# A gated long convolution and a SwiGLU layer on one core: the block convolution rewritten with four tokens per partition, the FFN weights kept in SBUF

## The chip, the cores and the metric

The kernel runs on one core of one Trainium2 chip. A core has several engines that run beside each other, each with its own queue of instructions in a fixed order, and they wait for one another through semaphores: TensorE (PE in the profile; its weight loads are listed as PEld), VectorE (DVE), ScalarE (ACT), GpSimd (POOL) and SyncE (SP). In this kernel SP and POOL only start transfers, apart from a few small memory fills on POOL. Matrix products land in PSUM, a small memory divided into banks, from which DVE or ACT carry the result to SBUF, the core's working memory; the inputs, the output and some intermediate arrays lie in DRAM.

The metric is the device time of one execution, in microseconds. Before the change the median of three runs is 397.13 us (397.08 to 398.56).

## The reference: what is computed

There are 2048 tokens of width D = 640 and an FFN of width F = 1728, all in bf16. With `x = A_q`:

```
k_shift[t] = sum over j in 0..3 of k[t-j] * shift_k[:, j]
kv   = k_shift * v
y    = causal convolution of kv along the tokens with ssm_k (2048 taps per channel)
y    = y + kv * ssm_D
h    = x + layernorm(x) * y
out  = h + (silu(n @ w_gate) * (n @ w_up)) @ w_down      with n = layernorm(h)
```

The reference writes the convolution with FFTs of length 4096. Both kernels cut the tokens into four blocks of 512 and the filter into four pieces of 512, transform each by a matrix product with a fixed table of cosines and sines, multiply the spectra of block j and filter piece p elementwise, add the products for output block i = j + p, and transform back by another matrix product. Ten (j, p) pairs are needed.

## The kernel before, in words

The program is written with a tile library: the text gives the operations in order and names buffers from pools; when the program is built, a scheduler puts the instructions of each engine into one fixed order. Where an operation's buffer is free and its operands are ready in the scheduler's own time, an operation that stands later in the text can go ahead of an earlier one. A buffer is free again when every reader of what it held is done.

*Filter pieces* (`g_piece`, L189). A piece is loaded, transposed on PE in sixteen rounds of five (L196), copied by ACT (L197) and transformed by `fwd_transform` (L147): eight groups of 4x2 matmuls of 320 columns (L153), each evacuated by ACT (L155). Pieces 1 to 3 are combined with the piece before by `hbuild` (L178, two DVE operations of 2560 elements a partition) and written to DRAM.

*Block front* (`conv_front_tiles`, L234). A block of 512 tokens is four tiles of 128 tokens, one token per partition. For each tile SP loads x, four copies of k shifted by 0 to 3 tokens (L250, L252; for the very first tile the shifted copies begin at partition 1, 2 or 3) and v. ACT takes the sums for the layer norm (L124, L125), DVE forms kv in eight operations of 640 elements (L257 to L262). `conv_front_finish` normalises x on ACT (L139) and transforms kv (L153).

*Products* (`cmac`, L157). A spectrum is 1024 coefficients by 640 channels, 8x640 elements per partition, and a pair is six or eight DVE operations of 2560 elements. The products go forward: as soon as the spectrum of block j exists, `pair(j, pp)` adds it to the accumulator of each later block; all accumulators stay in SBUF, and the filter spectra 1 to 3 are read back from DRAM (L226).

*Block back* (`conv_back`, L287). The inverse transform (L303) takes 16 matmuls of 320 columns per tile; DVE multiplies the PSUM result by the normalised x (L306) and adds x, loaded a second time (L313). h goes to DRAM (L314). ACT takes the sums of h, a square root (L134) and the normalisation (L139); PE transposes (L335) and ACT copies the result to hlnT (L336).

*FFN* (`ffn_quarter`, L338). POOL loads the gate and up weights again for each of the four blocks, in seven groups. For each of 14 chunks of up to 128 hidden units PE does five gate and five up matmuls of 512 columns (L356, L358) into one PSUM bank each; ACT makes the sigmoid, a copy of gate and a copy of up (L360 to L364), DVE two products (L366, L367). The down projection is 28 matmuls of 320 columns per tile (L376); DVE adds h, which POOL has loaded back from DRAM (L379, L381), and POOL stores the result (L382).

*Order in the text* (L384 to L405): front and back of block 0 with filter piece 0, pieces 1 to 3, then for k = 1, 2, 3: front of block k, back of block k, FFN of block k-1, the remaining forward products of block k-1; at last FFN 3. SP issues nearly all loads and the stores of spectra and h, in that order; POOL issues the FFN weights, h and the output.

Of the kernel before, what the change touches and what calls it, by code (L numbers as in the profile page):

```python
# [10 lines left out]
DEBUG_OUT = "out"  # L11

FP32 = mybir.dt.float32
BF16 = mybir.dt.bfloat16
ACT = mybir.ActivationFunctionType
# [3 lines left out]
D = 640  # L19
FF = 1728  # L20
P = 128
NT = S_TOT // P
MBLK = 512
NB = S_TOT // MBLK
TT_PER_BLK = MBLK // P
L = 2 * MBLK
NCOEF = 1024
NCT = NCOEF // P
EPS = 1e-5
NFCH = 14  # L30
GRP = 2
NGRP = NFCH // GRP
NH = 320


def make_basis():
    k = np.arange(MBLK)
    n = np.arange(MBLK)
    theta = 2 * np.pi * np.outer(k + 0.5, n) / L
    WF = np.concatenate([np.cos(theta), np.sin(theta)], axis=0).T.copy()  # L40
    WI = (2.0 / L) * np.concatenate([np.cos(theta), np.sin(theta)], axis=0)
    return WF.astype(np.float32), WI.astype(np.float32)
# [3 lines left out]
def kernel(  # L46
# [20 lines left out]
    cpool = ctx.enter_context(tc.tile_pool(name="cpool", bufs=1))  # L67
    ident_h = nc.inline_tensor(np.eye(P, dtype=np.float32).astype(ml_dtypes.bfloat16), name="const_ident")
    ident = cpool.tile([P, P], BF16, name="ident")
    nc.sync.dma_start(out=ident[:], in_=ident_h.ap())  # L70
    w4 = cpool.tile([P, 4, D], BF16, name="w4")
    with tc.tile_pool(name="tmpw", bufs=1) as tmpw:
        wbig = tmpw.tile([P, D, 4], BF16, name="wbig")
        nc.sync.dma_start(out=wbig[:], in_=A_shift_k.partition_broadcast(P))
        for j in range(4):
            nc.vector.tensor_copy(w4[:, j, :], wbig[:, :, j])
    wdp = ctx.enter_context(tc.tile_pool(name="wdp", bufs=1))
    freq = ctx.enter_context(tc.tile_pool(name="freq", bufs=1))
    blk = ctx.enter_context(tc.tile_pool(name="blk", bufs=1))
    iop = ctx.enter_context(tc.tile_pool(name="iop", bufs=2))  # L80
    ffq = ctx.enter_context(tc.tile_pool(name="ffq", bufs=1))
    wst = ctx.enter_context(tc.tile_pool(name="wst", bufs=2))
    ffio = ctx.enter_context(tc.tile_pool(name="ffio", bufs=2))
    small = ctx.enter_context(tc.tile_pool(name="small", bufs=2))
    dram = ctx.enter_context(tc.tile_pool(name="dram", bufs=1, space=bass.MemoryType.DRAM))
    psA = ctx.enter_context(tc.tile_pool(name="psA", bufs=2, space=bass.MemoryType.PSUM))
    psG = ctx.enter_context(tc.tile_pool(name="psG", bufs=1, space=bass.MemoryType.PSUM))
    psT = ctx.enter_context(tc.tile_pool(name="psT", bufs=2, space=bass.MemoryType.PSUM))
    gst0 = blk.tile([P, 5, MBLK], BF16, name="gst")
    nc.sync.dma_start(out=gst0[:], in_=A_ssm_k[0:D, 0:MBLK].rearrange("(dc p) t -> p dc t", p=P))  # L90

    WFnp, WInp = make_basis()
    WF_h = nc.inline_tensor(WFnp.astype(ml_dtypes.bfloat16), name="const_wf")
    WI_h = nc.inline_tensor(WInp.astype(ml_dtypes.bfloat16), name="const_wi")
    sgn_np = np.array([1.0 if (p % 2) == 0 else -1.0 for p in range(P)], dtype=np.float32).reshape(P, 1)
    sgn_h = nc.inline_tensor(sgn_np, name="const_sgn")
    nsgn_h = nc.inline_tensor((-sgn_np).astype(np.float32), name="const_nsgn")
    sgn_t = cpool.tile([P, 1], FP32, name="sgn_t")
    nc.sync.dma_start(out=sgn_t[:], in_=sgn_h.ap())
    nsgn_t = cpool.tile([P, 1], FP32, name="nsgn_t")  # L100
    nc.sync.dma_start(out=nsgn_t[:], in_=nsgn_h.ap())
    eps_t = cpool.tile([P, 1], FP32, name="eps_t")
    nc.vector.memset(eps_t[:], EPS)
    zero_t = cpool.tile([P, 1], FP32, name="zero_t")
    nc.vector.memset(zero_t[:], 0.0)
    Drow = cpool.tile([1, D], BF16, name="Drow")
    nc.sync.dma_start(out=Drow[:], in_=A_ssm_D.partition_broadcast(1))
    WF_t = cpool.tile([P, TT_PER_BLK, NCOEF], BF16, name="WF_t")
    WI_t = cpool.tile([P, NCT, MBLK], BF16, name="WI_t")

    wd_sb = wdp.tile([P, NFCH, D], BF16, name="wd_sb")

    h_dram = dram.tile([S_TOT, D], BF16, name="h_dram")
    hf_dram = dram.tile([NB, P, NCT, D], BF16, name="hf_dram")
    graw_dram = dram.tile([NB, P, NCT, D], BF16, name="graw_dram")

    Aacc = [freq.tile([P, NCT, D], BF16, name=f"Acc{i}") for i in range(NB)]
    Xcur = freq.tile([P, NCT, D], BF16, name="Xcur")
    Hld = [freq.tile([P, NCT, D], BF16, name=f"Hld{i}") for i in range(2)]
    Tprod = freq.tile([P, 4, D], BF16, name="Tprod")  # L120

    def ln_stats(x_tile: bass.AP, mv_out: bass.AP):
        junk = iop.tile([P, D], BF16, name="junk", bufs=1)
        nc.scalar.activation(junk[:], x_tile, ACT.Identity, bias=zero_t[:], scale=1.0, accum_out=mv_out[:, 0:1])  # L124
        nc.scalar.activation(junk[:], x_tile, ACT.Square, accum_out=mv_out[:, 1:2])  # L125

    def ln_finish_block(mvb: bass.AP, rb: bass.AP, nbb: bass.AP):
        T = mvb.shape[1]
        nc.vector.tensor_scalar(mvb[:, :, 0:1], mvb[:, :, 0:1], 1.0 / D, None, op0=ALU.mult)
        msq = small.tile([P, T, 1], FP32, name="ln_msq")  # L130
        nc.vector.tensor_mul(msq[:], mvb[:, :, 0:1], mvb[:, :, 0:1])
        nc.vector.scalar_tensor_tensor(mvb[:, :, 1:2], mvb[:, :, 1:2], 1.0 / D, msq[:], op0=ALU.mult, op1=ALU.subtract)
        sb = small.tile([P, T, 1], FP32, name="ln_sb")
        nc.scalar.activation(sb[:], mvb[:, :, 1:2], ACT.Sqrt, bias=eps_t[:], scale=1.0)  # L134
        nc.vector.reciprocal(rb, sb[:])
        nc.vector.scalar_tensor_tensor(nbb, mvb[:, :, 0:1], -1.0, rb, op0=ALU.mult, op1=ALU.mult)

    def ln_apply(x_tile: bass.AP, out_ap: bass.AP, rcol: bass.AP, nbcol: bass.AP):
        nc.scalar.activation(out_ap, x_tile, ACT.Identity, bias=nbcol, scale=rcol)  # L139

    def ps3(ps: bass.AP) -> bass.AP:
        return ps[:, :, 0:NH]

    def r3(ap2d: bass.AP) -> bass.AP:
        return ap2d.rearrange("p (a b) -> p a b", a=2)

    def fwd_transform(src4: bass.AP, dst8: bass.AP):  # L147
        for ct in range(NCT):
            ps = psA.tile([P, 2, 512], FP32, name="ps_mm")
            for kt in range(TT_PER_BLK):  # L150
                lhsT = WF_t[:, kt, ct * P:(ct + 1) * P]
                for h in range(2):
                    nc.tensor.matmul(ps[:, h, 0:NH], lhsT, src4[:, kt, h * NH:(h + 1) * NH],  # L153
# [35 lines left out]
    def g_piece(p: int, gst=None):  # L189
        if gst is None:  # L190
            gst = g_load(p)
# [244 lines left out]
```

## Time and profile before

| what | value |
|---|---|
| median of 3 runs | 397.13 us (397.08 to 398.56) |
| the profiled execution, first to last instruction | 397.7 us (no other time is listed for it) |
| mean granted TensorE clock | 0.955 |
| moved by DMA | 68.91 MB, mean 173 GB/s |
| first transform matmul / first FFN matmul / last matmul | 25.9 / 79.3 / 393.1 us |
| matmul records, weight loads | 1914, 1936 |

The profile page gives the busy time of each engine and the span in 40 slices of about 10 us, a digit being the busy share in tenths. A table by stages gives for each stretch of time the length, the busy time and number of instructions of PE, PEld, DVE, ACT and POOL, the mean granted clock, the DMA share and GB/s. In a timeline a line has the start, the length, the engine, the line of the program, the operation, output and inputs with their shape, and how many neighbours are merged. "128x640" is partitions by elements per partition; the engines' times follow the second number. "SPq" is SP's queue at work on issuing a transfer.

### The profile page before, as it was taken

How to read it: one execution, taken by the hardware profiler on the slowest of the kernel's cores; microseconds unless marked ns; L12 is line 12 of the kernel's file. 1: busy time of each engine (PE TensorE's matmuls, PEld its weight loads, DVE VectorE, ACT ScalarE, POOL GpSimd, SP SyncE). 2: the span in 40 equal slices, each digit the busy share in tenths (PEclk: the TensorE clock that was granted, in tenths of full speed). 3: DMA queues.
4: the chain of work that ended last, by engine and by line, in shares of the span. 5: the costliest groups of instructions: out<-in, count | busy, mean ns of one | idle time of the engine just before them, and what ended most of it. 6: DMA issues, size and time to landing. Idle time of an engine off the chain costs nothing.

```text
span 397.7 us, 5429 instructions
## 1 busy us (share of the span) xinstructions
PE 325.7 (82%) x1914; PEld 185.3 (47%) x1936; DVE 254.7 (64%) x413; ACT 253.8 (64%) x447; POOL 68.1 (17%) x95
## 2 busy tenths in 40 slices
PE   1038874497899779999779899897998999999995
PEld 1025542364567324565354355454534554544463
DVE  1185498500629989999949999983699723233321
ACT  1259607999786636479987539976664697166610
POOL 5000001000000303203102211131131111433121
PEclk9999969589999969999999999989999999999999
DMA  8589847513886996366863716351043332254111
GB/s 249 180 314 357 296 146 242 157 66 109 321 303 259 356 335 218 101 178 220 305 190 101 266 49 199 104 155 56 16 141 106 112 96 77 100 155 142 52 51 49
DMA packets 33610, 68.91 MB, mean 173 GB/s; under 512 B 4213, under 2 KB 25904, under 8 KB 31920
## 3 DMA queue, kind: packets, MB, share of 16 engines
q1 hardware_dynamic: 26800, 45.63, 33.7%
q0 software_dynamic: 6784, 22.94, 18.5%
q8 instruction: 15, 0.25, 0.2%
q14 instruction: 11, 0.09, 0.1%
HBM read 56.77 MB, written 11.80 MB: 172 GB/s over the span
## 4 chain that ended last, share of the span: by engine, by line
PE 33%; issue 25%; ACT 14%; DMA 13%; DVE 11%; SPq 2%; POOL 2%; POOLq 0%; DVEq 0%; ACTq 0%
PE ps_g L356 11%; PE ps_mm L376 7%; PE ps_mm L153 6%; PE ps_u L358 6%; PE ps_mm L303 4%; DMA wu_g<-in_B_w_up_dram 3%; ACT gc L362 3%; ACT xln_blk L139 3%; DMA k_148<-in_A_k_dram 2%; DMA wg_g<-in_B_w_gate_dram 2%; ACT junk L124 2%; SPq L250 2%; ACT sig L360 2%; DMA WF_t<-const_wf 1%; DMA wbig<-in_A_shift_k_dram 1%
## 5 line engine op out<-in xcount | busy, mean ns | idle before, releaser
L356 PE MATMUL ps_g<-hlnT,wg_g 128*128 128x512 bf16 (+1 forms) x268 | 70.9, 386 | 11.1 <-DMA wg_g<-in_B_w_gate_dram 6.1
L153 PEld LDWEIGHTS <-WF_t 128*128 128x128 bf16 x512 | 51.3, 101 | 48.7 <-DMA WF_t<-const_wf 13.8
L358 PE MATMUL ps_u<-hlnT,wu_g 128*128 128x512 bf16 (+1 forms) x270 | 70.3, 384 | 2.0 <-ACT uc L364 1.3
L376 PE MATMUL ps_mm<-wd_sb,tT 128*128 128x320 bf16 x448 | 69.6, 302 | 1.0 <-DVE tT L367 1.0
L360 ACT ACTIVATE sig<-ps_g 128x512 bf16<-128x512 f32 (+1 forms) x56 | 33.4, 597 | 50.0 <-PE ps_g L356 44.5
L376 PEld LDWEIGHTS <-tT 128*128 128x128 bf16 x448 | 41.9, 98 | 25.6 <-issue 7.1
L346 POOL DMA_DIRECT2D wg_g<-in_B_w_gate_dram x28 | 24.4, 873 | 168.9 <-PE ps_g L356 156.2
L153 PE MATMUL ps_mm<-gT,WF_t 128*128 128x320 bf16 x256 | 40.8, 313 | 15.1 <-DMA WF_t<-const_wf 13.5
L356 PEld LDWEIGHTS <-wg_g 128*128 128x128 bf16 (+1 forms) x280 | 27.3, 99 | 47.4 <-issue 14.7
L153 PE MATMUL ps_mm<-kv_blk,WF_t 128*128 128x320 bf16 x256 | 39.0, 307 | 6.9 <-ACT Xcur L155 3.9
L358 PEld LDWEIGHTS <-wu_g 128*128 128x128 bf16 (+1 forms) x280 | 27.5, 99 | 34.6 <-issue 3.7
L366 DVE TENSOR_TENSOR gs<-gc,sig 128x512 bf16<-128x512 bf16 (+1 forms) x56 | 23.2, 419 | 30.3 <-ACT gc L362 30.3
L364 ACT CAST uc<-ps_u 128x512 bf16<-128x512 f32 (+1 forms) x56 | 32.8, 586 | 10.8 <-DVE tT L367 3.3
L303 PEld LDWEIGHTS <-WI_t 128*128 128x128 bf16 x256 | 25.8, 102 | 17.5 <-issue 5.3
L362 ACT CAST gc<-ps_g 128x512 bf16<-128x512 f32 (+1 forms) x56 | 32.6, 582 | 0.0
L348 POOL DMA_DIRECT2D wu_g<-in_B_w_up_dram x28 | 24.4, 871 | 34.1 <-PE ps_u L358 21.5
L367 DVE TENSOR_TENSOR tT<-gs,uc 128x512 bf16<-128x512 bf16 (+1 forms) x56 | 23.2, 419 | 7.3 <-ACT uc L364 7.0
L155 ACT CAST Xcur<-ps_mm 128x640 bf16<-128x640 f32 x32 | 21.7, 693 | 9.0 <-PE ps_mm L153 9.0
L124 ACT ACTIVATE junk<-h_t,zero_t 128x640 bf16<-128x640 bf16 x16 | 13.2, 828 | 21.8 <-DVE h_t L313 21.5
L261 DVE TENSOR_TENSOR kv_blk<-kv_blk,ktmp 128x640 bf16<-128x640 bf16 x48 | 23.4, 487 | 0.8
L124 ACT ACTIVATE junk<-x_t,zero_t 128x640 bf16<-128x640 bf16 x16 | 13.3, 831 | 13.0 <-DMA x_t<-in_A_q_dram 12.7
L382 POOL DMA_DIRECT2D out_dram<-o_t x16 | 8.8, 553 | 65.4 <-DVE o_t L381 52.0
(256 smaller groups left out, 412.7 us busy)
## 6 DMA issues: line engine op xcount, KB each, us to landing
wg_g<-in_B_w_gate_dram POOLq DMA_DIRECT2D x24, 320.0 KB, 3.6
wu_g<-in_B_w_up_dram POOLq DMA_DIRECT2D x24, 320.0 KB, 4.2
Hld_129<-hf_dram SPq DMA_DIRECT2D x3, 1280.0 KB, 5.5
Hld_130<-hf_dram SPq DMA_DIRECT2D x3, 1280.0 KB, 9.9
gst<-in_A_ssm_k_dram SPq DMA_DIRECT2D x4, 640.0 KB, 7.7
x_t<-in_A_q_dram SPq DMA_DIRECT2D x16, 160.0 KB, 5.4
v_t<-in_A_v_dram SPq DMA_DIRECT2D x16, 160.0 KB, 3.9
h_dram<-h_t SPq DMA_DIRECT2D x16, 160.0 KB, 2.7
```

The source lines that it names most:

```text
L124: nc.scalar.activation(junk[:], x_tile, ACT.Identity, bias=zero_t[:], scale=1.0, accum_out=mv_out[:, 0:1])
L153: nc.tensor.matmul(ps[:, h, 0:NH], lhsT, src4[:, kt, h * NH:(h + 1) * NH], start=(kt == 0), stop=(kt == TT_PER_BLK - 1))
L261: nc.vector.tensor_add(ks, ks, tmp[:])
L303: nc.tensor.matmul(ps[:, h, 0:NH], lhsT, Acc[:, ct, h * NH:(h + 1) * NH], start=(ct == 0), stop=(ct == NCT - 1))
L346: nc.gpsimd.dma_start(out=wg_g[:, :, 0:ncols], in_=B_w_gate[:, f0:f0 + ncols].rearrange("(kt p) f -> p kt f", p=P))
L348: nc.gpsimd.dma_start(out=wu_g[:, :, 0:ncols], in_=B_w_up[:, f0:f0 + ncols].rearrange("(kt p) f -> p kt f", p=P))
L356: nc.tensor.matmul(ps_g[:csz, :], wg_g[:, kt, off:off + csz], hlnT[:, kt, :], start=(kt == 0), stop=(kt == 4))
L358: nc.tensor.matmul(ps_u[:csz, :], wu_g[:, kt, off:off + csz], hlnT[:, kt, :], start=(kt == 0), stop=(kt == 4))
L360: nc.scalar.activation(sig[:csz, :], ps_g[:csz, :], ACT.Sigmoid)
L362: nc.scalar.copy(gc[:csz, :], ps_g[:csz, :])
L364: nc.scalar.copy(uc[:csz, :], ps_u[:csz, :])
L376: nc.tensor.matmul(ps_o[:, h, 0:NH], lhsT, wd_sb[:csz, c, h * NH:(h + 1) * NH], start=(c == 0), stop=(c == NFCH - 1))
```

## The change

The computation is the same; nearly all of the code is new. Lines of the new kernel, cut to what the text speaks of:

```diff
+    spp = pool("spp", 6)
+    ldp = pool("ldp", 4)
+    hp = pool("hp", 2)
+    psg = pool("psg", 3, space=bass.MemoryType.PSUM)
+    psm = pool("psm", 2, space=bass.MemoryType.PSUM)
+    pst = pool("pst", 1, space=bass.MemoryType.PSUM)
...
+    def kv_loads(b, hf):
...
+        kt = kvp.tile([P, 7, NH], BF16, name="kt")
+        if b == 0:
+            nc.gpsimd.memset(kt[0:1, 0:3, :], 0.0)
+            nc.sync.dma_start(out=kt[:, 3:7, :], in_=kk[0:BLK, d0:d0 + NH].rearrange("(p j) d -> p j d", j=4))
+            nc.sync.dma_start(out=kt[1:P, 0:3, :], in_=kk[0:BLK - 4, d0:d0 + NH].rearrange("(p j) d -> p j d", j=4)[:, 1:4, :])
+        else:
+            src = bass.AP(tensor=kk.tensor, offset=kk.offset + (r0 - 3) * D + d0, ap=[[4 * D, P], [D, 7], [1, NH]])
+            nc.sync.dma_start(out=kt[:], in_=src)
...
+    def fwd_split(src, dst):
+        eo = spp.tile([P, 2, 4, NH], BF16, name="eo", tag="sp")
+        for par in range(2):
+            for c in range(2):
+                ps = psm.tile([P, 2, 512], FP32, name="ps_f", tag="mm")
+                for q in range(2):
+                    for j in (par, par + 2):
+                        nc.tensor.matmul(ps[:, q, 0:NH], fwd_w(j, 0, c * 2 + q), src[:, j, :],
+                                         start=(j == par), stop=(j == par + 2))
+                nc.scalar.copy(eo[:, par, c * 2:c * 2 + 2, :], ps[:, :, 0:NH])
+        nc.vector.tensor_add(dst[:, 0:4, :], eo[:, 0], eo[:, 1])
+        nc.vector.tensor_sub(dst[:, 4:8, :], eo[:, 0], eo[:, 1])
...
+        nc.vector.tensor_scalar(rb.bitcast(I32), var[:].bitcast(I32), -0.5, 1597463007.0, op0=ALU.mult, op1=ALU.add)
+        for _ in range(3):
+            nc.vector.tensor_mul(t[:], rb, rb)
...
+    def g_transform(p, gst, dst2):
+        gT = hp.tile([P, NJ, D], BF16, name="gT", tag="xln")
...
+    def conv_half(b, hf):
...
+        kv = kv_make(b, hf, kvt[b, hf])
+        xc = spp.tile([P, 8, NH], BF16, name="xc", tag="sp")
+        if b == 0:
+            fwd_dense(kv, xc)
+        else:
+            fwd_split(kv, xc)
+        if b < NB - 1:
+            nc.gpsimd.dma_start(out=x_dr[b][hf], in_=xc[:])
+        acc = spp.tile([P, 8, NH], BF16, name="acc", tag="sp")
+        for j in range(b):
+            xl = ldp.tile([P, 8, NH], BF16, name="xl", tag="ld")
+            nc.sync.dma_start(out=xl[:], in_=x_dr[j][hf])
+            hl = ldp.tile([P, 8, NH], BF16, name="hl", tag="ld")
+            nc.sync.dma_start(out=hl[:], in_=h_dr[b - j][hf])
+            pair(acc, xl, hl, first=(j == 0))
+        pair(acc, xc, h0[hf], first=(b == 0))
+        xln = xln_b[b]
+        if b > 0:
+            ee = t2p.tile([P, 4, NH], BF16, name="ee", tag="t2")
+            nc.vector.tensor_add(ee[:], acc[:, 0:4, :], acc[:, 4:8, :])
+            nc.vector.tensor_sub(acc[:, 4:8, :], acc[:, 0:4, :], acc[:, 4:8, :])
...
+            nc.vector.tensor_scalar(hln[:], h_t[:, j, :], rb[:, j, :], nbb[:, j, :], op0=ALU.mult, op1=ALU.add)
...
+    def ffn(b):
...
+        for c in range(NC_FULL):
...
+            ps_g = psg.tile([P, BLK], FP32, name="ps_g", tag="gu")
...
+            ps_u = psg.tile([P, BLK], FP32, name="ps_u", tag="gu")
...
+            with tc.high_priority():
+                nc.scalar.activation(sil[:], ps_g[:], ACT.Silu)
+                nc.scalar.copy(uc[:], ps_u[:])
+                nc.vector.tensor_mul(tT[:, c, :], uc[:], sil[:])
...
+            if not last:
+                for h in range(2):
+                    nc.tensor.matmul(ps_o[:, h, 0:NH], ident[:], h_t[:, m, h * NH:(h + 1) * NH], start=True, stop=False)
...
+    for p in range(1, NB):
+        cur = [spp.tile([P, 8, NH], BF16, name="gc", tag="sp") for hf in range(2)]
+        g_transform(p, gt, cur)
+        h_build(p, cur, prev)
+        prev = cur
+        if p < NB - 1:
+            gt = g_load(p + 1)
+        if p == 1:
+            x_load(1)
+            ln1(1)
+            for hf in range(2):
+                conv_half(1, hf)
+            ln2(1)
+            ffn(0)
+    for b in range(2, NB):
+        x_load(b)
+        ln1(b)
+        for hf in range(2):
+            conv_half(b, hf)
+        ln2(b)
+        ffn(b - 1)
+    ffn(NB - 1)
```

What it does, part by part (the number in a pool is how many buffers a tag of it has):

- The tag `sp` (six buffers) holds raw filter pieces, even and odd halves, spectra and accumulators; `ld` (four) the spectra read back; `xln` (two) the transposed filter pieces and the normalised x, which turns into h in place and stays until the block's FFN has used it. Gate and up share three PSUM banks, transposes have one.
- In `conv_half`, `kv_make` and each of its products are DVE operations of 1280 elements (`pair`: six for the first product of a block, else eight). The full forward or inverse transform of a half takes 32 matmuls, the split one 16.
- A block's token 4p + j lies on partition p, place j. One load brings the seven k rows that a partition needs, and the width is worked in two halves of 320 (`hf`), each with its own transforms, products and inverse.
- The frequencies are shifted by a quarter step instead of a half. The upper half of the 512 complex frequencies then has the table of the lower half, with the sign of odd places j turned. `fwd_split` transforms even and odd places separately with half the matmuls and forms their sum and difference on DVE; the inverse likewise (`ee`). Block 0 and all filter pieces use the full form.
- The products go backward: block b reads the spectra of earlier blocks and of the filter pieces from DRAM when it needs them. Only piece 0's spectrum stays in SBUF.
- The gate, up and down weights are loaded once, by SP; the left-over 64 gate and up columns share one group of five matmuls. Stores of spectra (`h_build` for the filter pieces) and of the output go through POOL. Silu replaces sigmoid, copy and one product. h stays in SBUF; for blocks 0 to 2 it is added by two matmuls with the identity.
- The normalisation's inverse root is made by 15 small DVE operations (three Newton steps), h is normalised on DVE, and the four shift weights are copied apart by ACT.
- In the text, FFN 0 now stands before filter pieces 2 and 3.

## The prediction

> **What bounds the kernel now.** I read the page's busy times and the row of 40 slices first, then the engines' busy time stage by stage, then start-to-start distances in the timeline, because a mean duration of pipelined instructions overlaps its neighbours.
>
> ```profile
> span 397.7 us, 5429 instructions
> ...
> PE 325.7 (82%) x1914; PEld 185.3 (47%) x1936; DVE 254.7 (64%) x413; ACT 253.8 (64%) x447; POOL 68.1 (17%) x95
> ...
> PE   1038874497899779999779899897998999999995
> ```
>
> PE is nearly full from slice 8 on and thin before. By stages (cut where the first FFN matmul starts, 79.3, and where FFN 3 takes over, 338):
>
> ```profile
> 0.00:79.30 79.30, 39.00 (x243) 25.62 (x245) 45.44 (x96) 42.82 (x78) 6.63 (x13) 0.89 0.75 243
> 79.30:130.00 50.70, 46.40 (x330) 31.22 (x334) 19.74 (x17) 41.23 (x67) 1.74 (x2) 0.97 0.57 210
> 130.00:190.00 60.00, 54.13 (x301) 28.32 (x303) 57.67 (x81) 38.06 (x73) 13.70 (x18) 0.94 0.68 234
> 190.00:260.00 70.00, 60.31 (x348) 32.49 (x350) 64.06 (x103) 54.35 (x95) 13.25 (x16) 1.00 0.54 175
> 260.00:338.00 78.00, 71.12 (x398) 39.10 (x404) 50.47 (x85) 54.12 (x96) 16.51 (x22) 0.96 0.31 93
> ```
>
> After the window come PE, PEld, DVE, ACT and POOL busy, the granted clock, DMA share and GB/s. The first 79 us are latency (PE 39 of 79). After them PE does 287 us in the 314 us up to its last matmul (393.1): PE is the bound, and DVE is as dense from 130 to 260 (122 of 130). Prices:
>
> ```profile
> 121.10 8.86 PE L153 MATMUL ps_mm<-kv_blk,WF_t 128*128 128x320 bf16 x64
> ...
> 347.58 1.24 PE L356 MATMUL ps_g<-hlnT,wg_g 128*128 128x512 bf16 x5
> 348.65 1.24 PE L358 MATMUL ps_u<-hlnT,wu_g 128*128 128x512 bf16 x5
> ...
> 349.98 1.24 PE L356 MATMUL ps_g<-hlnT,wg_g 128*128 128x512 bf16 x5
> ...
> 288.75 1.48 DVE L173 TENSOR_TENSOR Tprod<-Xcur,Hld_130 128x2560 bf16<-128x2560 bf16 x1
> 290.15 0.42 DVE L367 TENSOR_TENSOR tT<-gs,uc 128x512 bf16<-128x512 bf16 x1
> ...
> 4.84 0.30 SPq L250 DMA_DIRECT2D k_142<-in_A_k_dram  x1
> 5.96 6.31 SPq L250 DMA_DIRECT2D k_145<-in_A_k_dram  x1
> ...
> 18.79 0.49 DVE L260 TENSOR_TENSOR ktmp<-k_142,w_60 128x640 bf16<-128x640 bf16 x1 [6.19 <-DMA k_142<-in_A_k_dram]
> ```
>
> A 320-column matmul takes 0.136 (8.7 us for 64); a 512-column one 0.215, but an FFN chunk of ten takes 2.40 (347.58 to 349.98): 0.25 is a wait for the one ps_g bank. DVE's 2560-element operation has a pace of 1.40 (288.75 to 290.15); the page's mean of a 640-element one is 487 ns (L261) against 1482 for 2560 (L172, by shape), 0.52 ns an element, so 640 pace at 0.40 and 1280 at 0.73. Busy times of back-to-back operations overlap by about 0.08, so I add paces, not means.
>
> **The change part by part.**
>
> *PE.* Before: 56 chunks x 2.40 = 134; 448 down, 512 forward and 256 inverse matmuls x 0.136 = 165; 160 transposes (five in 0.29) 9: 309. After: 540 x 0.215 = 116 (three banks and two evacuations of 0.59 per 2.15; if the wait stays, 130); down 448 plus 24 identity matmuls 64; forward 256 for the filter and 64 + 3x32 for kv, 57; inverse 64 + 3x32, 22; transposes 9: 268 (to 281). PE loses 28 to 41. The filter's transposes read every fourth column; the nearest row is the flat one (121 ns a load), twice that on 80 loads is +10 at worst, beside DVE work.
>
> *DVE.* Before, in paces: kv 128x0.40 = 51, products 72x1.40 = 101, filter build 6x2.88 = 17, y and output 32x0.74 = 24, residual 6, FFN 112x0.335 = 38, LN 8: 245 (page: 254.7). After: kv 64x0.73 = 47, products 144x0.73 = 105, even/odd sums 24x0.73 = 18, filter build 12x0.73 = 9, y 12, residual 6, FFN 56x0.335 = 19, output 3, normalising h 16x0.40 = 6, the iterated root 120 small operations x0.2 = 24: 249. DVE does not shrink. Unseen: multiplying by a broadcast row. Flat price 0.73 against the pace of the 640-element PSUM form doubled (1.48): 32x0.75 = +24 at worst; I take flat, the runs being 320 contiguous elements; flat is also the low end, since no row shows a faster form. Normalising h lies between a 4-element operation (0.16) and a 640-element copy (0.49).
>
> *ACT.* One pass less per chunk, 56x0.59 = -33; the h normalisation 16x0.82 = -13; 14 of 15 table loads x1.28 = -18; output copies 12x0.69 = +8, shift-weight copies +3: 254 becomes 201. Unseen: Silu, taken as Sigmoid's 597 ns; if it needed a reload at each of 16 changes to LN, +20 and still no bound. [...]
>
> *DMA and queues.* Weights are loaded once, not four times (-13 MB), k in one overlapping load, q once; spectra go out and back (24 MB against 17). 68.9 becomes about 47 MB. SP issues some 64 transfers instead of 154 at about 0.4 us, POOL 28 instead of 88 at 0.55 to 0.87. New on SP: a spectrum load that waits for one of four slots holds the next half's k, v and q loads behind it. New on POOL: spectrum stores stand between output stores, and an early output store that waits for its FFN would hold a spectrum store, and through it a later block's load. The round trip of h through memory goes; POOL's waits for it (56 us, once) were beside everything else, so this gains nothing. The residual's 24 identity matmuls take DVE's output additions of blocks 0 to 2 to ACT.
>
> *Start.* Block 0's k loads end on 127 partitions, twice, 127x3 rows of 640 B = 244 KB each. The nearest row is k_142, 127 partitions, 158.8 KB: issued at 4.84, awaited until 18.79, and the next issue on SP took 6.31. At its 11.4 GB/s each new one takes 21 us; at 21 GB/s (free when SP moved on, 12.31) 11.6. Issue at 3.5 plus both is 27 to 46; I take 35, because k_142 moved beside 1.3 MB of FFN weights that no longer come so early. Then for half 1: kv 7x0.73 = 5.1, forward 4.4 + copy 0.7, products 4.4, inverse 4.4, y and residual 2.2, h statistics 4x1.95 = 7.8, root 3, four rounds of normalise, transpose and copy through one bank (two before) 4x1.5 = 6, and 3 for the lower clock (0.69 here before). FFN 0 starts at 76, against 79.3: no gain. [...]
>
> *From FFN 0 to FFN 3.* This is the wait that the change adds. The tag xln now gives two slots to four transposed filter pieces and four normalised blocks. Piece 2 takes the slot that block 0's h leaves, at the end of FFN 0: 76 + 45 (29 + 16) + 6 for block 1's inverse and transposes = 127. Pieces 2 and 3 (2x12: 64 matmuls, 20 transposes, copies) reach 151, and only then have block 2's products both operands and accumulator slots (six slots of tag sp, of which two pieces' spectra and two raw pieces hold up to six). Behind the waiting copy of piece 2 on ACT and PE nothing needed earlier is queued; who waits is DVE. The single hT and tT slots wait as their counterparts did before. DVE work at hand until then: rest of block 1 25, FFN 0 5, kv 2 12, LN 6, build 6 = 54 of 75 us. Left: block 2 43, block 3 66 (kv 12, 60 products 44, sums 6, y 4), FFN 1 and 2 9, LN 9 = 127. PE's FFN 1 and 2 (90) and transforms (22) fit beside that. So block 3 ends at 278 with DVE full, 289 at the 92% it held between 130 and 260; I take 280, since kv 3 can fill earlier gaps. Then LN of h 17 (as above), FFN 3 45 and 4.6 from last matmul to end (393.1 to 397.7): 346.6. That is against this execution's own 397.7; the median shown is 397.1, so 346.
>
> **Rivals.**
>
> *A: the slots do not bite* (piece 2 finds a slot earlier, or products run ahead). For it: PE's 268 less the 44 done by 76 (pieces 0 and 1, block 0, block 1's forward half, 60 transposes) is 224, at the 91% density of before 246: 76 + 246 + 5 = 327. Against: the two slots are in the code.
>
> *B: spectra arrive late.* Twelve pairs load 1.3 MB each for 5.9 us of products. The reloads of 1280 KB landed in 5.5 us in one group, 9.9 in the other. At 9.9 each pair waits 4: +48, less some 12 in gaps: 382. For it: 9.9; against: the DMA share is 0.3 to 0.5 after 190 and falls.
>
> *C, slower: FFN no longer lies beside the convolution*, because an engine's order, fixed at build, puts transforms waiting for DVE ahead of ready FFN matmuls. All three exposed would be 3x45 = +135, 481. It decides from 51 of the 135 us uncovered. Against: before, L356 and L303 alternate within a block.
>
> *D: the half transforms buy nothing.* They save PE 192 matmuls, 26 us, and charge DVE 18. Where DVE sets the pace, as I say, the full form would be faster; this lies inside the forecast.
>
> **How the numbers follow.** Main case 0.45, A 0.25, B 0.15, C 0.12, between B and C 0.03. Forecast 346. A with the early start (327 less 9) gives the low end, 318; B with some of the broadcast price the high end, 388. Faster by over 0.5% 0.85, within 0.5% (about what a measurement can tell) 0.02, slower 0.13.
>
> **What would show it.** Right: DVE near 250 and PE near 270 busy; first FFN matmul at 65 to 85; the first k loads landing after 30; DVE idle ahead of block 2's products with the third filter piece beginning at FFN 0's end; FFN chunks at 2.15. Wrong: DVE waiting mainly for spectrum loads (B), a gapless PE (A), PE waiting for copies of a transform while FFN matmuls are ready (C), products at well over 0.73.

## The result, and the profile after

The changed kernel takes 446.25 us (445.83 to 447.78), the kernel before beside it 397.54: a ratio of 1.120, 95% interval 1.116 to 1.125. Slower by 12%, where 346 was forecast. The sums of work of DVE, ACT and the transfers came out as forecast, PE's higher (303.1 busy, where the prediction's signs had near 270); above all, the work doesn't lie side by side. The page of the profiled execution:

```profile
span 443.8 us, 4672 instructions
...
PE 303.1 (68%) x1732; PEld 171.1 (39%) x1748; DVE 251.8 (57%) x466; ACT 206.1 (46%) x370; POOL 17.2 (4%) x34
...
PE   0074676049998259999995404999962306999995
...
DVE  0310487442499794332499799645998796311121
...
PEclk9995988759999859999998555999996556999998
```

PE is 22.6 us less busy than before (325.7), and 46 us longer on its way. Read the PE and DVE rows one above the other, with the slices (11.1 us each) numbered from 0: in 15 to 19 PE is at 9 and DVE at 2 to 4, in 21 to 24 DVE is at 7 to 9 and PE at 0 to 5, in 30 to 32 again DVE at 7 to 9 and PE at 0 to 3. They take turns, and in slices 22 to 24, 31 and 32, where PE is at 0 to 4, the PEclk row is at 5.

Busy time by stages, cut at the first FFN matmul (98.2), the gate matmuls of FFN 1 (184.3), FFN 2 (296.7) and FFN 3 (393.4); columns as in the stages of before (PE, PEld, DVE, ACT, POOL, granted clock, DMA share, GB/s):

```profile
0.00:98.20 98.20, 41.22 (x237) 26.19 (x239) 38.34 (x81) 43.40 (x82) 3.15 (x8) 0.84 0.61 199
98.20:184.30 86.10, 70.83 (x419) 39.92 (x423) 57.70 (x107) 50.17 (x90) 3.77 (x7) 0.91 0.29 96
184.30:296.70 112.40, 84.28 (x500) 48.77 (x505) 76.33 (x134) 58.25 (x107) 5.39 (x10) 0.83 0.34 120
296.70:393.39 96.69, 61.67 (x334) 32.79 (x335) 70.18 (x126) 37.04 (x68) 2.17 (x4) 0.81 0.17 62
393.39:443.80 50.41, 45.10 (x245) 23.48 (x247) 9.27 (x18) 17.25 (x29) 2.71 (x5) 0.98 0.05 17
```

From FFN 0 to FFN 3 (98.2 to 393.4, 295.2 us) PE is busy for 70.83 + 84.28 + 61.67 = 216.8, or 73%; before it was 232 of 258.7 there, 90%. DVE is busy for 204.2. So PE idles 78 us and DVE 91 us in the same stretch. The forecast had this stretch at 221 us (76 to 297): 74 of the 97 us that the execution lies over the forecast's 346.6 are here, 22 in the start, 1 in FFN 3.

PE's timeline at the places where it waits for DVE, lines picked out:

```profile
134.06 1.26 PE L312 MATMUL ps_y<-ee,wi 128*128 128x320 bf16 x8 [0.69 <-DVE ee L304]
...
142.57 1.24 PE L363 MATMUL ps_gu<-hT,wl 128*128 128x512 bf16 x5
...
159.81 2.31 PE L312 MATMUL ps_y<-ee,wi 128*128 128x320 bf16 x8 [12.06 <-DVE ee L304]
...
164.58 4.24 PE L379 MATMUL ps_o<-wd,tT 128*128 128x320 bf16 x28
...
271.94 2.31 PE L312 MATMUL ps_y<-ee,wi 128*128 128x320 bf16 x8 [15.87 <-DVE ee L304]
...
296.16 0.72 PE L171 MATMUL ps_f<-kv,wf 128*128 128x320 bf16 x4
...
370.19 2.31 PE L312 MATMUL ps_y<-ee,wi 128*128 128x320 bf16 x8 [21.99 <-DVE ee L304]
```

FFN 0's last gate and up group (L363) is issued at 142.6. Its down projection (L379) could follow from 146 on, when DVE has made its last input, and doesn't: PE waits 12 us at the inverse of block 1's second half, and down comes after it. The same at 272 and 370, with 16 and 22 us. Behind down stand the next block's forward transforms (L171, 296.2), and behind those the sums and most of the products that DVE has for that block.

The start, SP's queue. The k loads on partitions 1 to 127 are L124; "SPq" with 11.13 is SP held while it issues the next transfer:

```profile
1.89 0.51 SPq L124 DMA_DIRECT2D kt<-in_A_k_dram  x1
2.45 11.13 SPq L129 DMA_DIRECT2D vt<-in_A_v_dram  x1
...
18.24 12.84 SPq L129 DMA_DIRECT2D vt<-in_A_v_dram  x1
31.12 0.89 SPq L265 DMA_DIRECT2D x_t<-in_A_q_dram  x1
```

x is issued at 31, so block 0's normalisation, inverse, statistics and FFN 0 (first matmul 98.2) come late. DVE stands at the statistics of x until 49.8, and the second half's kv (L140), behind them in DVE's order, begins at 56.6:

```profile
49.76 0.17 DVE L211 TENSOR_SCALAR mean<-stat 128x4 f32<-128x4 f32 x1 [25.66 <-ACT junk L225]
...
56.60 0.81 DVE L140 TENSOR_TENSOR kv<-kt,w 128x1280 bf16<-128x1280 bf16 x1
```

### The profile page after: what moved, and what is told of

It reads as the page before. It is cut to its first block, busy times and chain, and to the rows that moved or that the text cites. A ratio compares the mean times of both kernels' runs of the same rounds, so it can differ in the third digit from the quotient of the medians.

```text
span 443.8 us, 4672 instructions
## 1 busy us (share of the span) xinstructions
PE 303.1 (68%) x1732; PEld 171.1 (39%) x1748; DVE 251.8 (57%) x466; ACT 206.1 (46%) x370; POOL 17.2 (4%) x34
## 3 DMA queue, kind: packets, MB, share of 16 engines
q1 hardware_dynamic: 25758, 37.24, 25.7%
## 4 chain that ended last, share of the span: by engine, by line
issue 59%; DVE 11%; PE 11%; DMA 6%; ACT 4%; SPq 3%; POOL 3%; POOLq 0%; DVEq 0%; ACTq 0%
PE ps_f L160 4%; DMA kt<-in_A_k_dram 4%; SPq L129 3%; PE ps_y L316 3%; POOL out_dram L387 2%; DMA x_t<-in_A_q_dram 2%; DMA gst<-in_A_ssm_k_dram 1%; PE ps_y L312 1%; DVE acc L201 1%; PE ps_o L379 1%; DVE prod L200 1%; ACT junk L225 1%; ACT eo L173 1%; DVE kv L144 1%; DVE tT L359 1%
## 5 line engine op out<-in xcount | busy, mean ns | idle before, releaser
L379 PE MATMUL ps_o<-wd,tT 128*128 128x320 bf16 x448 | 67.2, 301 | 0.0
L350 PE MATMUL ps_g<-hT,wg 128*128 128x512 bf16 x250 | 65.5, 383 | 0.7 <-issue 0.2
L353 PE MATMUL ps_u<-hT,wu 128*128 128x512 bf16 x254 | 64.9, 379 | 0.1
L312 PE MATMUL ps_y<-ee,wi 128*128 128x320 bf16 x48 | 12.3, 427 | 59.3 <-DVE ee L304 59.3
L379 PEld LDWEIGHTS <-tT 128*128 128x128 bf16 x448 | 42.2, 98 | 20.6 <-issue 5.0
L160 PE MATMUL ps_f<-gT,wf 128*128 128x320 bf16 x256 | 42.7, 321 | 8.6 <-ACT h L162 7.9
L359 DVE TENSOR_TENSOR tT<-uc,sil 128x512 bf16<-128x512 bf16 x52 | 21.9, 420 | 44.6 <-ACT uc L358 44.6
L160 PEld LDWEIGHTS <-wf 128*128 128x128 bf16 x320 | 32.3, 103 | 27.2 <-issue 10.6
L357 ACT ACTIVATE sil<-ps_g 128x512 bf16<-128x512 f32 x52 | 31.2, 600 | 19.8 <-PE ps_g L350 18.3
L358 ACT CAST uc<-ps_u 128x512 bf16<-128x512 f32 x52 | 30.6, 588 | 20.3 <-PE ps_u L353 19.8
L350 PEld LDWEIGHTS <-wg 128*128 128x128 bf16 x260 | 25.5, 99 | 28.9 <-issue 1.1
L353 PEld LDWEIGHTS <-wu 128*128 128x128 bf16 x260 | 25.4, 98 | 28.4 <-issue 0.2
L173 ACT CAST eo<-ps_f 128x640 bf16<-128x640 f32 x24 | 16.3, 704 | 34.4 <-PE ps_f L171 34.4
L171 PE MATMUL ps_f<-kv,wf 128*128 128x320 bf16 x96 | 19.9, 356 | 16.3 <-DVE kv L145 15.5
L240 PE MATMUL ps_t<-ident,gst 128*128 128x128 bf16 x80 | 8.5, 247 | 22.9 <-DMA gst<-in_A_ssm_k_dram 20.9
L171 PEld LDWEIGHTS <-wf 128*128 128x128 bf16 x96 | 10.5, 113 | 25.8 <-DVE kv L145 17.1
L338 PE MATMUL ps_t<-ident,hln 128*128 128x128 bf16 x80 | 8.1, 241 | 17.2 <-DVE hln L335 14.9
```

What stands on the lines that cost most here:

```text
L160: nc.tensor.matmul(ps[:, q, 0:NH], fwd_w(j, hi, c * 2 + q), src[:, j, :], start=(j == 0), stop=(j == NJ - 1))
L171: nc.tensor.matmul(ps[:, q, 0:NH], fwd_w(j, 0, c * 2 + q), src[:, j, :], start=(j == par), stop=(j == par + 2))
L173: nc.scalar.copy(eo[:, par, c * 2:c * 2 + 2, :], ps[:, :, 0:NH])
L312: nc.tensor.matmul(ps[:, i, 0:NH], wi_f[:, c, j, :], rhs, start=(c == 0), stop=(c == 3))
L350: nc.tensor.matmul(ps_g[:], wg_sb[:, kt, f0:f0 + P], hT[:, kt, :], start=(kt == 0), stop=(kt == 4))
L353: nc.tensor.matmul(ps_u[:], wu_sb[:, kt, f0:f0 + P], hT[:, kt, :], start=(kt == 0), stop=(kt == 4))
```

## The experiments

Ratios are to the kernel before, measured beside each, with 95% intervals. A "point" is 1% of its time, 4 us.

**One cause at a time.** Three suspects from the profile: the place of the down projection, the slot named in the prediction, the k loads.

`down_gu`: down in the gate/up banks.

```diff
-            ps_o = psm.tile([P, 2, 512], FP32, name="ps_o", tag="mm")
+            for h in range(2):
+                ps_o = psg.tile([P, BLK], FP32, name="ps_o", tag="gu")
```

> The down projection's sums move from the two-bank tag mm, which they share in the order of the text with the transforms of the convolution, to single banks of the gate/up tag (two halves of 320 columns, one after the other); nothing else changes. Theory 1 (down of block b-1 stands behind block b's inverse transforms, which wait for DVE's products, and the next block's forward transforms stand behind that down): PE's idle time at the second inverse of blocks 1 to 3 (12, 16 and 22 us) is filled by the 18 us of down, the forward transforms of block 3 follow their input at once (14 us earlier), and the whole falls by 25 to 50 us, to 396 to 421. Theory 2 (block 2 waits for the normalised block's slot, through the transposed filter pieces) and theory 3 (late start by the 127-partition loads): PE's waits move but DVE's idle stretch at 160 to 220 and the first 98 us stay; under 10 us, 436 to 446.

Measured: 428.5 us, 1.077 (1.072 to 1.083), 4.3 points less than the change's 1.120. The direction of theory 1, less than it asked. PE's timeline of this kernel shows down (L379) around the second inverse instead of behind it:

```profile
160.34 2.17 PE L379 MATMUL ps_o<-wd,tT 128*128 128x320 bf16 x14
...
162.59 1.25 PE L312 MATMUL ps_y<-ee,wi 128*128 128x320 bf16 x8
...
178.06 0.71 PE L338 MATMUL ps_t<-ident,hln 128*128 128x128 bf16 x5 [8.89 <-DVE hln L335]
```

But then down no longer covers block 1's statistics, and PE waits 8.9 us there. In the whole run PE's waits for the sums before an inverse fall from 59.3 to 10.8 us, and those for the normalised h (L338) rise from 14.9 to 41.4: much of the gain turns into the next wait.

`gt_ld`: the slot.

```diff
-        gT = hp.tile([P, NJ, D], BF16, name="gT", tag="xln")
+        gT = ldp.tile([P, NJ, D], BF16, name="gT", tag="ld")
```

> The transposed filter pieces take a slot of the spectrum loads' tag instead of one of the two slots of the normalised blocks; nothing else changes. Theory 2 (the step of the prediction from FFN 0 to FFN 3: pieces 2 and 3 wait for FFN 0's end because of that slot, and DVE has nothing to do until then): the pieces run before FFN 0's end at 183, block 2's products begin 20 to 40 us earlier, 405 to 425. Theory 1: the pieces stand behind the down projection and the statistics of block 1 on PE and in the transform banks whatever the slot; no more than 5 us, 441 to 447.

Measured: 446.0 us, 1.121 (1.115 to 1.127): nothing. Filter piece 2 (L240) still begins at 182, right behind the transposes of block 1's h (L338):

```profile
180.79 0.44 PE L338 MATMUL ps_t<-ident,hln 128*128 128x128 bf16 x5
181.07 1.22 PE L379 MATMUL ps_o<-wd,tT 128*128 128x320 bf16 x7
182.22 0.47 PE L240 MATMUL ps_t<-ident,gst 128*128 128x128 bf16 x5
```

Both use the one transpose bank, in the order of the text. The loads that use the tag `ld` are read by block 1's products, and those are done when its last inverse starts (158.9); so a slot was free, and nothing came earlier. That the bank is what holds the piece is read from these lines; no run has a second bank.

`kload`: the 127-partition loads split in two.

```diff
-  out=kt[1:P, 0:3, :]
+  out=kt[1:16, 0:3, :]
+  out=kt[16:P, 0:3, :]
```

> Block 0's overlapping k load on partitions 1 to 127 is split into partitions 1 to 15 and 16 to 127, twice; nothing else changes. Theory 3 (SP is held 11.1 and 12.8 us behind these loads, so x comes at 38 and FFN 0's first matmul at 98): FFN 0 begins near 76 and the end moves by as much, 20 us, to 426. Theory 1: what follows FFN 0 is set by DVE and the order on PE, and the 20 us stay nearly whole since everything is shifted; 424 to 432. If the load is hidden anyway: 444 to 447.

Measured: 427.5 us, 1.074 (1.068 to 1.079), 4.7 points. As theory 3 says: SP is free at once, x is issued at 9.3, FFN 0 begins at 79.4.

```profile
1.90 0.65 SPq L124 DMA_DIRECT2D kt<-in_A_k_dram  x1
2.59 0.35 SPq L125 DMA_DIRECT2D kt<-in_A_k_dram  x1
2.98 0.55 SPq L130 DMA_DIRECT2D vt<-in_A_v_dram  x1
...
9.34 0.62 SPq L266 DMA_DIRECT2D x_t<-in_A_q_dram  x1
```

```profile
37.58 0.82 DVE L141 TENSOR_TENSOR kv<-kt,w 128x1280 bf16<-128x1280 bf16 x1
```

```profile
79.38 1.91 PE L351 MATMUL ps_g<-hT,wg 128*128 128x512 bf16 x4 [0.22 <-issue]
```

`all3`, the three together:

> The three edits together: down projection in the gate/up banks, filter pieces in a slot of the spectrum loads, the k load split. If the three causes add up: 20 from the start, 25 to 50 from the order on PE, some 10 more from the slot once PE's order is free: 370 to 400. If the down projection's place is not the cause: 415 to 426.

Measured: 410.4 us, 1.031 (1.024 to 1.038). The two effects add up (8.9 points) and no more; still slower than before. DVE still idles while the filter pieces 2 and 3 run (busy for 18.9 of the 40 us from 140 to 180).

**The order of the filter pieces.** `ord` moves pieces 2 and 3 ahead of block 1's convolution:

```diff
     for p in range(1, NB):
         ...
-        if p == 1:
-            x_load(1)
-            ... (block 1, FFN 0)
+    x_load(1)
+    ... (block 1, FFN 0)
```

> On the changed kernel the order of the text alone: filter pieces 1, 2 and 3 come one after the other before block 1's convolution, instead of pieces 2 and 3 after block 1's statistics and FFN 0. Theory 4 (not the slot but the text's order keeps pieces 2 and 3 back: their transposes stand behind block 1's in the one transpose bank, so DVE has no products of block 2 from 160 to 220): DVE's idle time there goes, block 1's products begin some 24 us later, block 2's follow without a gap; the down projection still waits for the inverse, so the end moves by 10 to 25, to 421 to 436. If PE's work in that stretch sets the time anyway (it is full there): 440 to 450.

Measured: 447.6 us, 1.122 (1.118 to 1.125): nothing. DVE's idle time moves: from 180 to 220 it is busy for 28.1 us instead of 12.9, from 100 to 140 for 11.3 instead of 25.7, and PE's near-empty slices move behind it. `all4e` adds the order to `all3`, with piece 1 ahead of block 0's second statistics:

> The three edits of all3 (410.4) and the order: piece 1 of the filter before block 0's second statistics, pieces 2 and 3 right after, block 1's convolution behind them. Theory 4: of DVE's 75 us of idle time between 60 and 340 in all3, the 25 at 160 to 200 go and part of the 24 at 60 to 100; block 3 ends at 295 to 310 instead of 342, the whole 360 to 380. If only PE's total counts (307 busy, 75% of the span): under 10 us, 400 to 410.

Measured: 396.1 us, 0.992 (0.988 to 0.995). The order is worth 4 points here. `ord` alone, which lacks the move of piece 1 and so is not quite the same edit, gave nothing. Why it takes the other edits is not shown; it may be that while the transforms and down still take turns with DVE, an earlier filter piece only waits elsewhere.

**The half transforms.** `all4ed` is `all4e` with full transforms in every block:

```diff
-        if b == 0:
-            fwd_dense(kv, xc)
-        else:
-            fwd_split(kv, xc)
+        fwd_dense(kv, xc)
...
-        if b > 0:      # ee, acc sums; inverse from ee and acc
+        if b < 0:
```

> all4e with the full transforms for blocks 1 to 3 as well, forward and inverse, in place of the even and odd halves and the 24 sums on DVE. Theory D of the prediction (where DVE sets the pace the halves buy nothing; 18 us of DVE against 26 us of PE): 5 to 12 us less than all4e. If PE sets the pace: 10 to 20 more.

Measured: 375.6 us, 0.942 (0.939 to 0.945): 5 points (20 us) less, more than the 5 to 12 us expected by rival D, though PE has 192 matmuls more. `dense` is the same edit on the changed kernel, alone:

> On the changed kernel one edit alone: full transforms for all blocks, forward and inverse, instead of even and odd halves with their 24 sums. all4ed against all4e: 20 less. Theory E (the half form costs by its chain: copies on ScalarE, sums on DVE, then products, and sums again before the inverse, each time where DVE's products set the end): the same here, 15 to 25 less, 421 to 431, since here too PE waits for the sums (12, 16 and 22 us at the second inverse of a block). Theory D of the prediction (only 18 us of DVE against 26 us of PE): 0 to 10 less, 436 to 446.

Measured: 415.8 us, 1.039 (1.034 to 1.045): 8.1 points, the largest single effect. One half of it at a time, `fwd_full` and `inv_full`:

> On the changed kernel: the forward transforms full, the inverse in halves as the change has it. Theory E1 (the forward half's own cost: the extra tile eo takes one of the six slots of tag sp, so the second half of a block can't be transformed while the first is in its products, and its copies and sums stand between PE and the products): most of the 30, 422 to 428. Theory D (DVE's time alone): half of the 18, 434 to 440.

> On the changed kernel: the inverse full, the forward transforms in halves as the change has it. Theory E2 (the sums before the inverse make PE wait 59 us in all, six times): 12 to 20 less, 426 to 434. Theory E1: under 9 us less, 438 to 446. Theory D: 434 to 440.

Measured: 416.5 us, 1.046 (1.043 to 1.049) with the forward transforms full, 441.2 us, 1.107 (1.105 to 1.110) with the inverse full. The forward half carries 7.4 of the 8.1 points. Is it the time of its sums? `dense_pad` puts four sums per half back, off the chain:

```diff
         pair(acc, xc, h0[hf], first=(b == 0))
+        if b > 0:
+            for i in range(4):
+                ex = t2p.tile([P, 4, NH], BF16, name="ex", tag="t2")
+                nc.vector.tensor_add(ex[:], xc[:, 0:4, :], xc[:, 4:8, :])
```

> The kernel with full transforms (415.8) with four more sums of 1280 elements on DVE for each half of blocks 1 to 3, as many as the half transforms had, written to a scratch tile that nothing reads. Theory D (DVE's time at the end of each block): 24 x 0.73 more, 430 to 434. Theory E1 (chain and slot): 416 to 424.

Measured: 421.9 us, 1.060 (1.057 to 1.063). DVE's 18 us cost 2.1 points, 8 us: a quarter of the 8.1. Is it the extra buffer? `eo_t2` takes two others, from the tag `t2`, which holds five scratch tiles:

```diff
-        eo = spp.tile([P, 2, 4, NH], BF16, name="eo", tag="sp")
+        eo = [t2p.tile([P, 4, NH], BF16, name="eo", tag="t2") for _ in range(2)]
```

> On the changed kernel: eo as two tiles of the tag t2 (the products' scratch) instead of one slot of tag sp; the half transforms stay. If the slot costs the forward half's 25 us beyond its DVE time: 418 to 426. If the chain does (copies on ScalarE, sums on DVE, then the products): 440 to 446.

Measured: 442.7 us, 1.107 (1.102 to 1.112): 1.3 points, less whatever the two tiles cost the products in `t2`. What is left by subtraction, some 4 to 5 points, is put down to the chain itself: PE, copies on ACT, sums on DVE, and only then the products. PE's waits for the sums before the inverse go with it (us in all, times, longest), in the changed kernel, in `fwd_full` and in `eo_t2`:

```profile
PE ps_y L312 <- DVE ee L304: 59.3, 6, 22.0
...
PE ps_y L309 <- DVE ee L301: 32.0, 6, 17.6
...
PE ps_y L312 <- DVE ee L304: 61.1, 6, 23.9
```

Without the forward halves 27 us of waiting go; with another buffer none do. In `dense` and `dense_pad` PE waits 28.8 and 29.0 us for the products before the inverse (block 0's 3.5 among them), so the added sums don't bring the waits back either. The timelines of ACT and DVE in the changed kernel show the chain at block 3:

```profile
304.60 0.93 ACT L278 ACTIVATE xln<-x_t,nbb,rb 128x640 bf16<-128x640 bf16 x1
...
305.90 0.59 ACT L358 CAST uc<-ps_u 128x512 bf16<-128x512 f32 x1
306.37 0.72 ACT L173 CAST eo<-ps_f 128x640 bf16<-128x640 f32 x1
```

```profile
307.11 0.83 DVE L174 TENSOR_TENSOR xc<-eo 128x1280 bf16<-128x1280 bf16 x1 [0.17 <-ACT eo L173]
307.86 0.82 DVE L175 TENSOR_TENSOR xc<-eo 128x1280 bf16<-128x1280 bf16 x1
308.59 0.82 DVE L190 TENSOR_TENSOR acc<-xl,hl 128x1280 bf16<-128x1280 bf16 x1
```

PE finished the forward transform at 300.5. Its last copy (L173) stands on ACT behind the normalisation of x and FFN 2's passes until 306.4; the sums (L174, L175) wait for it, and behind the sums in DVE's order stands the product L190, which reads spectra of earlier blocks and no transform at all. Products of this kind that write scratch tiles run before (from 279.4 on); L190 is the first that writes the accumulator. In `eo_t2`, where the halves take no buffer of the accumulator's tag, it stands behind the sums too (304.8). Why the scheduler puts it there no run shows. In `fwd_full` the same product starts before the forward transform has ended:

```profile
282.31 0.82 DVE L190 TENSOR_TENSOR acc<-xl,hl 128x1280 bf16<-128x1280 bf16 x1
```

That is 25.2 us after the start of block 2's last inverse (257.1) instead of 36.6 (271.9 to 308.6): 11.5 us at this place. In `eo_t2` it is 31.9 (272.9 to 304.8). Whether the sums would be cheap with the ready products written ahead of them was not tried.

**What the final version needs.** Three reductions of `all4ed`: without the order (`all3d`), without the new place of down (`no_down`), without the slot (`dko`).

> all4ed with the order of the text as the change has it (filter pieces 2 and 3 after FFN 0): down projection in the gate/up banks, the slot, the k load split, full transforms. If the order is worth what it was between all3 and all4e (410.4 to 396.1): 388 to 392. If with full transforms PE is full anyway: 375 to 380.

> all4ed with the down projection back in the two-bank tag mm of the transforms, all else as in all4ed. Theory 1 (down of block b-1 stands behind block b's inverse): its 18 us are exposed again at blocks 1, 2 and 3, partly beside the statistics of the second normalisation: 18 to 40 more than all4ed, 393 to 415. If the early filter pieces and full transforms already fill PE: 375 to 382.

> all4ed with the transposed filter pieces back in the two slots that the normalised blocks use (the change's own slots). The step of the prediction that named these two slots: the pieces share one slot while block 0's holds the other, and block 1's normalised copy waits for them; if that binds once the rest is mended, 5 to 15 more than all4ed, 380 to 390. If the slots never bind: 374 to 378.

Measured: 394.7 us, 0.989 (0.985 to 0.993); 375.6 us, 0.939 (0.935 to 0.943); 375.1 us, 0.939 (0.935 to 0.942). The order is worth 4.7 points here. The place of down, worth 4.3 in the changed kernel, is worth nothing here: in `no_down` PE waits about 1 us at the second inverse of blocks 1 and 2, where it waited 12 and 16, and only at block 3's still 12. `kod` leaves both of the latter out:

> The k load split, the filter pieces ahead of block 1's convolution (piece 1 before block 0's second statistics) and full transforms, without the two edits that made no difference at the end (down projection in other banks, another slot). If both are without effect together too: 374 to 377. If one covers for the other: 380 to 395.

Measured: 374.7 us, 0.940 (0.936 to 0.944). `kofd` keeps the inverse halves and has the split load, the order, full forward transforms and down in the gate/up banks:

> The k load split, the filter pieces early, forward transforms full, down projection in the gate/up banks, but the inverse in halves as the change has it. Against the 375 of kod: PE has 96 matmuls fewer (13 us), DVE 12 sums more (9). If PE sets the time there, as its rows say: 362 to 372. If the sums before the inverse cost as in inv_full (5): 376 to 384.

Measured: 370.1 us, 0.926 (0.921 to 0.930), 7.4% faster than before and the fastest version. Against `all4ed`, from which it differs by the inverse halves and by the slot, which has no effect, it is 1.6 points faster. Against `all4e` it differs by the forward transforms and the slot: 6.6 points. Its page and its stretch from FFN 0 to FFN 3:

```profile
span 367.5 us, 4891 instructions
...
PE   0695769359999999997999989999899921899994
...
DVE  3306878441336999989999998599999944021221
```

```profile
80.65:315.01 234.36, 210.99 (x1279) 119.97 (x1278) 188.13 (x352) 141.04 (x263) 10.76 (x20) 0.96 0.33 113
```

PE is busy for 211.0 of 234.4, 90% as in the kernel before. In slices 13 to 31 PE is at 7 to 9 and DVE, but for one 5, at 8 and 9.

**Silu alone.** `b_silu` is the kernel before with Silu:

```diff
-                nc.scalar.activation(sig[:csz, :], ps_g[:csz, :], ACT.Sigmoid)
+                nc.scalar.activation(sig[:csz, :], ps_g[:csz, :], ACT.Silu)
-                (the copy gc, the product gs)
-                nc.vector.tensor_mul(tT[:csz, c, :], gs[:csz, :], uc[:csz, :])
+                nc.vector.tensor_mul(tT[:csz, c, :], uc[:csz, :], sig[:csz, :])
```

> The kernel before with one part of the change alone: Silu in place of Sigmoid, the copy of the gate sum and the product with it. If the wait of 0.25 us per chunk for the one gate bank goes, since the bank is read once instead of twice: 56 x 0.25, 8 to 14 us less than 397, 383 to 389. If the saved passes only lay beside PE: 395 to 398.

Measured: 389.9 us, 0.975 (0.969 to 0.980). A chunk takes 2.16 there (346.80 to 348.95) with one gate bank, so the wait of 0.25 was for the bank's second reader, and three banks are not needed for that; 9 to 10 of the 14 us arrive.

## Why the prediction was wrong

*What held.* DVE 251.8 busy (249 in paces), ACT 206.1 (201; 13 table loads went, not 14), 48.0 MB (47), the 1280-element operation 0.73 to 0.74 from start to start, multiplying by a broadcast row flat at that pace, FFN chunks at 2.16 (2.15), FFN 3 with its tail 50.4 (49.6). Spectrum loads were not what DVE waited for (1.6 us in all), so rival B is out. *What did not:* PE was to be busy near 270 and is for 303.1; the sum of 268 is in paces, and by the ratio of before (325.7 busy, 309 in paces) it would be 282 in the profile's count. The rest goes with the waits: the 96 matmuls of the split inverse take 24.6 us here and 15.0 in `kofd`, where PE idles for 23 us from FFN 0 to FFN 3 instead of 78. The first FFN matmul came at 98.2, not at 65 to 85. And DVE's "92% between 130 and 260" is 121.7 of 130, 94%, which makes 287 of the 289 and decides nothing.

*The step that failed* is the sentence "PE's FFN 1 and 2 (90) and transforms (22) fit beside that". It compared two sums of work and took the smaller as hidden. In the text all products of a block stand between its forward transform and its inverse, although those with earlier blocks' spectra need neither, and PE and DVE overlap only if the order on each engine lets other ready work in between. Often it didn't: 78 us of PE's idle time lie between FFN 0 and FFN 3, where the forecast's 221 us would leave four beside the 216.8 that PE was busy. From the end of filter piece 3 (212.2) to the end of block 3's convolution (375.7) it took 163.5 us, and the forecast had 129 (151 to 280).

The term before it was short by as much: "45 (29 + 16) + 6", 51 us from FFN 0's first matmul to filter piece 2, was 85.6 (98.2 to 183.8). It has nothing for filter piece 1, which PE works from 97.3 to 112.1, nor for block 1's forward transforms, nor for the 12 us of waiting at its second inverse. These two stretches are 69 of the 74 us.

In kind this is rival C, which was to decide from 51 us uncovered: down stands behind an inverse that waits for DVE. By `down_gu` that is worth 4.3 of the 12 points, so its price of 481 was too high, and its chance of 0.12 too low. A share as large (the 4 to 5 points left by subtraction) has the same form on DVE's side, where ready products stand behind the sums of the half transforms; rival C did not name it. What spoke against C, the alternation of L356 and L303 before, didn't carry over. It may have held because the forward products of the kernel before stood ready for DVE; no run tests that.

*The start* was the other miss. "Issue at 3.5 plus both" put both k loads side by side in SP's queue. One took 16.5 us (issued 1.89, DVE goes on at 18.34), inside the 11.6 to 21 taken; but SP was held for 11.1 us behind it, so the second was issued at 17.1, and x, which the sum didn't contain, behind another 12.8. The rest of the chain was sized right: from the second half's kv to FFN 0 the sum has 41 us, and it takes 41.6 in the changed kernel (56.6 to 98.2) and 41.8 in `kload` (37.6 to 79.4). But that kv doesn't begin when its k has landed, as the sum has it. In DVE's order it stands behind the statistics of x and the first half's products, and in `kload`, where x and all of block 0's k and v are issued by 10, it still begins at 37.6. The sum has nothing for that, so that 79.4 comes near its 76 is luck: k, issued by 8.5 and landing in some 6 us, comes about 20 us earlier than its 35. While the first load on 127 partitions is under way and little else moves, the DMA share of the changed kernel (the last but one number) is 0.07, at 21 GB/s.

```profile
7.00:13.00 6.00, 0.00 (x0) 0.00 (x0) 0.00 (x0) 0.86 (x2) 0.00 (x0) 1.00 0.07 21
```

From its issue to DVE's going on, this load, 238 KB, took 16.5 us (14.8 GB/s). Split into 28 and 210 KB, in `kload`, it lands in 6.0 and 6.1 us. Why the one transfer takes so much longer no run shows.

*The slot* (tag xln) was named as "the wait that the change adds". The third piece did begin at FFN 0's end and DVE did idle before block 2, as the list of signs asked; but the cause was another. Another slot changed nothing, in the changed kernel and in the mended one. The order of the text holds the piece back: in `ord`, with the slots as they were, it begins at 112.6, in the middle of FFN 0's gate and up matmuls. The one transpose bank is how it does so, by the reading above. A sign that fits two causes decides nothing.

*Rival D* had the right sign and was too small: where DVE sets the pace the full form would be faster, by no more than the 18 us that the halves charge DVE, which "lies inside the forecast". They cost 8.1 points, 32 us, of which 8 is DVE's time by `dense_pad`. The prediction priced the sums as work and not as a link between PE and the products. In the fastest version, where PE is 90% busy, the inverse halves are a gain of 1.6 points.

*What remains open:* `kofd` is 24 us over the forecast of 346. PE has 23 us of idle time between FFN 0 and FFN 3, 12 of them at block 3's statistics ahead of FFN 3, and FFN 0 starts at 80.7; no run separates these further.

## What to carry to other kernels

A sum per engine is a lower bound, not a forecast: where two engines hand work to each other several times per block, write down for each hand-over what else stands ready behind it in the waiting engine's fixed order, and count every microsecond for which the answer is "nothing". Halving the matmuls with two extra sums was a bad trade here where the sums stand between the transform and the work that sets the pace, and a fair one behind it. Remove one suspect at a time and then all together: here two edits that gave 4% each gave 9 together, two others gave nothing alone (one of them, in a fuller form, 4% later), and one of the 4% was worth nothing once the rest was mended.

## What the runs showed of the hardware

In the changed kernel the first eight 320-column matmuls of a split inverse take longer after a longer wait: 1.26 us after 0.69 (134.06), 1.78 after 3.77 (331.57), 2.31 after 4.87 (241.11) and 2.31 after 12.06, 15.87 and 21.99 (159.81, 271.94 and 370.19). The granted clock is 0.50 in whole stretches such as this one, with PE busy for 4.45 of 20 us:

```profile
340.00:360.00 20.00, 4.45 (x16) 2.24 (x16) 16.75 (x24) 2.77 (x4) 0.00 (x0) 0.50 0.18 66
```

From 7 to 13, where PE has no instruction at all, it is 1.00 (the row from 7.00 to 13.00, at the start's k loads). What lowers the clock, and after how long a wait, no run shows. The mean granted clock is 0.859 in the changed kernel, 0.925 with full transforms (`dense`) and 0.947 in `kofd`.

The loads on 127 partitions also held the queue that issued them: the next transfer on SP took 11.1 and 12.8 us to issue, against 0.55 behind the same rows split at partition 16.
